# One pool for every tile, u through SyncE, and the first logits mixed with the last inverse in an attention-plus-S4 kernel

## The chip, the cores and the metric

The kernel runs on one core of a Trainium2 chip. Its time is device microseconds of one execution. The core has TensorE (PE; PEld is its weight load), VectorE (DVE), ScalarE (ACT), GpSimd (POOL) and SyncE (SP), each with an instruction stream of its own, and 16 DMA engines. DMAs are issued here from the queues of SyncE, ScalarE and GpSimd.

## What is computed

Two independent parts share one output of 2048 x 1280; the left 640 columns come from A, the right 640 from B.

```python
# A: local dilated attention; H = 32 heads of Dh = 20, window W = 8, dilation 2
q, k, v = split(x @ wqkv)                  # x 2048 x 640, wqkv 640 x 1920
idx = pos[:, None] - 2 * arange(8)[None]   # masked where negative
logits = einsum("hsd,hswd->hsw", q, k[idx]) * Dh ** -0.5
o = einsum("hsw,hswd->hsd", softmax(logits), v[idx])
a = o @ wo
# B: S4 convolution; D = 640 channels, N = 192 states, L = 2048
dt = exp(log_dt)
K[d, l] = real(sum_n C[d, n] * exp(dt[d] * A[d, n] * l) * dt[d] * B[d, n])
y = irfft(rfft(pad(u)) * rfft(pad(K)))[:L] + u * Dskip
```

## The kernel before, in words

Part B goes by five chunks of 128 channels (NCH = 5, 32 channels in each of four groups). For each chunk the coefficients are brought into base, log magnitude and phase (`prep_coef`, `prep_chunk`), written to a scratch in DRAM (`scr`) and read back transposed as "pieces" PF and PM (`load_pieces`). `table_steps` multiplies the pieces with constant matrices RF and RM, and ACT turns the results into tables of sines and exponentials Y and X; `kgen_steps` multiplies Y with X into the convolution kernel (tile Ksb). Each chunk does this in two halves, th = 0 and 1. `fwd_steps` is a two-step FFT by matmuls (f1 with BD, f2 with WU for u or WK for the kernel), run for u (`u_steps`, result stored to Udram) and for Ksb. `inv_steps` reloads u's spectrum as U and Uw, multiplies it with the kernel's (`prod`, L425) and makes the first step of the inverse (`ia`, L434) into Z. The second step, `ib` (L574), needs the Z of all five chunks: four are stored to Zdram and read back into the 40 KB tile Zall, the fifth is written there directly. It starts each PSUM tile with u times Dskip through an identity matmul, and puts the result where u was, from where two DMAs of four parts store it.

Steps are Python closures; `interleave` mixes two lists evenly. A scheduler of the framework then orders each engine's instructions by that order and by its own estimate of when they become ready; the result is a fixed stream for each engine. `InOrder` pins chains by hand: `order` on ACT, `vorder` on DVE, `sorder` on SyncE's loads of pieces and constants. PSUM has eight banks: in part B one tile "w" of two banks for the FFT steps (one buffer), "tb" of two banks (two buffers) for tables, "k" of one bank (two buffers).

Part A: `headA` loads x, transposes it with matmuls (L638) and projects the keys (L646), both beside the last inverse and `ib`. After part B's pools close, `partA` projects half the queries (L673), then mixes the logits of that half (DVE products at L695, matmuls at L698) with the projection of the values (L682), projects the other half of the queries, makes the first softmax (L716 to L733) and the second half's logits, then the weighted values (DVE L749, matmuls L753) and the output projection (L765). An item of logits takes eight window offsets w for one half of each 512 positions.

SBUF is divided into pools that open and close: `bbase` (u, WK, IA, H), `tabc`, `piece`, `tabA`, `prep`, then `tabB`, `a_h`, `zall`, `a_w`, `a_s`. A pool that opens in the place of a closed one waits until the closed one's tiles are done.

At the start ACT's queue issues log_dt (L51), two coefficient loads (L487), BD and the four parts of u (L492); the Exp of log_dt (L59) follows them in ACT's stream, and all coefficient work follows that Exp.

Of the kernel before, what the change touches and what calls it, by code (L numbers as in the profile page):

```python
# [44 lines left out]
def load_dt(tc, pools, prm):  # L45
    nc = tc.nc
    pool = pools["bbase"]
    ldt = pool.tile([128, NCH], bf16, name="ldt")
    lsrc = prm["B_log_dt"].rearrange("(g c t) -> g t c", g=4, c=NCH, t=32)
    for g in range(4):  # L50
        nc.scalar.dma_start(out=ldt[32 * g:32 * g + 32, :], in_=lsrc[g])  # L51
    return ldt


def prep_dt(tc, pools, ldt, order):
    nc = tc.nc
    pool = pools["bbase"]
# [9 lines left out]
def prep_coef(tc, pools, nat, lndt, n, order, vorder, pool, sfx):  # L67
# [5 lines left out]
    T = pool.tile([128, 5, n, CW], f32, name="cf" + sfx)  # L73
# [11 lines left out]
    def logs():  # L85
        order(nc.scalar.activation(out=T[:, 2:5], in_=T[:, 2:5], func=ACT.Ln, bias=pools["tiny"][:]))
        V.tensor_tensor(out=T[:, 3], in0=T[:, 3], in1=T[:, 2], op=A.subtract)
        V.scalar_tensor_tensor(out=T[:, 2], in0=T[:, 3], scalar=-1.0, in1=T[:, 3], op0=A.mult, op1=A.max)
        V.scalar_tensor_tensor(out=T[:, 4], in0=T[:, 4], scalar=0.5, in1=lndt.unsqueeze(2).to_broadcast(W), op0=A.mult, op1=A.add)
        order(nc.scalar.activation(out=T[:, 2], in_=T[:, 2], func=ACT.Exp, scale=-0.5))  # L90
        nc.scalar.activation(out=T[:, 3], in_=T[:, 3], func=ACT.Sign)
        nc.scalar.activation(out=T[:, 0:2], in_=T[:, 0:2], func=ACT.Sign, bias=pools["tiny"][:])
# [7 lines left out]
    return zed, logs, angle, T[:, 4], T[:, 2]  # L100


def prep_chunk(tc, pools, Are, Aim, dts, lam, ang, c, scr, vorder):
# [4 lines left out]
    pool = pools["prep"]  # L108
    st = {}

    def frac(out, x, q):
        tk = pool.tile([128, CW], f32, name="tk", tag="tk", bufs=2)
        V.tensor_scalar(out=tk[:], in0=x, scalar1=1.0 / q, scalar2=MAGIC, op0=A.mult, op1=A.add)
        V.tensor_scalar(out=tk[:], in0=tk[:], scalar1=MAGIC, scalar2=q, op0=A.subtract, op1=A.mult)
        V.tensor_tensor(out=out, in0=x, in1=tk[:], op=A.subtract)

    def base():
        b1 = st["b1"] = pool.tile([128, 3, CW], f32, name="b1", tag="b1", bufs=2)
        pc = pool.tile([128, 6, CW], f16, name="pc1", tag="pc1")
        tq = pool.tile([128, CW], f32, name="tq", tag="tq", bufs=2)  # L120
        first = V.tensor_scalar(out=b1[:, 1], in0=Are, scalar1=dts[:, 0, c:c + 1], scalar2=-60000.0, op0=A.mult, op1=A.max)
        second = V.tensor_scalar(out=tq[:], in0=Aim, scalar1=dts[:, 1, c:c + 1], scalar2=None, op0=A.mult)
        frac(b1[:, 0], tq[:], 65536.0)
        frac(b1[:, 2], b1[:, 0], 1024.0)
        nc.scalar.copy(out=pc[:, 0:3], in_=b1[:])
        vorder(first)
        vorder(second)
        lastop = V.tensor_tensor(out=pc[:, 3:6], in0=b1[:], in1=pc[:, 0:3], op=A.subtract)
        vorder(lastop)
        nc.sync.dma_start(out=scr[c, 0:6].rearrange("k p n -> p k n"), in_=pc[:])  # L130

    def logmag():
        pc = pool.tile([128, 2, CW], f16, name="pc2", tag="pc2")
        nc.scalar.copy(out=pc[:, 0], in_=lam)
        vorder(V.tensor_tensor(out=pc[:, 1], in0=lam, in1=pc[:, 0], op=A.subtract))
        nc.sync.dma_start(out=scr[c, 6:8].rearrange("k p n -> p k n"), in_=pc[:])

    def phi():
        tq = pool.tile([128, CW], f32, name="tq", tag="tq", bufs=2)
        b2 = pool.tile([128, CW], f32, name="b2", tag="b2")  # L140
        pc = pool.tile([128, 2, CW], f16, name="pc3", tag="pc3")
        V.tensor_scalar(out=tq[:], in0=st["b1"][:, 0], scalar1=31.5, scalar2=None, op0=A.mult)
        V.scalar_tensor_tensor(out=tq[:], in0=ang, scalar=-TURN, in1=tq[:], op0=A.mult, op1=A.add)
        frac(b2[:], tq[:], 65536.0)
        nc.scalar.copy(out=pc[:, 0], in_=b2[:])
        V.tensor_tensor(out=pc[:, 1], in0=b2[:], in1=pc[:, 0], op=A.subtract)
        nc.sync.dma_start(out=scr[c, 8:10].rearrange("k p n -> p k n"), in_=pc[:])
# [3 lines left out]
def new_pieces(tc, pools):  # L151
# [3 lines left out]
    PF = pools["piece"].tile([128, 8, CW], f16, name="PF", tag="PF")  # L155
    PM = pools["piece"].tile([128, 8, CW], f16, name="PM", tag="PM")
# [36 lines left out]
def table_steps(tc, pools, R, P, th, order, Y, X, rows=(128, 128), vorder=None):  # L193
# [8 lines left out]
    pool, psp = pools["tab"], pools["psum"]  # L202
# [129 lines left out]
def const_tile(tc, pool, arr, name, eng, dt=bf16, order=None):  # L332
    t = pool.tile(list(arr.shape), dt, name=name)
    ins = eng.dma_start(out=t[:], in_=tc.nc.inline_tensor(arr if dt == bf16 else arr.astype(np.float16), name="c_" + name).ap())
# [34 lines left out]
def fwd_steps(tc, pools, BD, W, src_fn, banks, ev1, ev2, each=None, done=None):  # L369
# [3 lines left out]
    pool = pools["fwd"]  # L373
# [31 lines left out]
def inv_steps(tc, pools, IA, Ud, banks, ev, done, zdst=None):  # L405
# [3 lines left out]
    pool = pools["inv"]  # L409
# [17 lines left out]
    def ia(q):  # L427
        def run():
            if q == 0:
                st["Z"] = zdst[0] if zdst is not None else pool.tile([128, 128, 32], bf16, name="Z", tag="Z")[:]  # L430
# [5 lines left out]
            if q == 3 and done is not None:  # L436
# [5 lines left out]
def partB(tc, pools, prm, B_u, B_Dskip, out_b, open_head):  # L442
# [4 lines left out]
    with ExitStack() as outer:  # L447
        opened = lambda name, **kw: outer.enter_context(tc.tile_pool(name=name, **kw))
        dpool = opened("dram", bufs=1, space=bass.MemoryType.DRAM)
# [3 lines left out]
        psk = opened("psum_k", bufs=2, space=bass.MemoryType.PSUM)  # L453
        bbase = opened("bbase", bufs=1)
        fwp = opened("fwd", bufs=1)
        ivp = opened("inv", bufs=1)
        short = ExitStack()
        tcp = short.enter_context(tc.tile_pool(name="tabc", bufs=1))
        pcp = short.enter_context(tc.tile_pool(name="piece", bufs=2))
        tabA = short.enter_context(tc.tile_pool(name="tabA", bufs=1))  # L460
        pools.update(psum=psk, bbase=bbase, piece=pcp, fwd=fwp, inv=ivp, tab=tabA)
        order = InOrder(tc)
        vorder = InOrder(tc)
        sorder = InOrder(tc)
        tiny = bbase.tile([128, 1], f32, name="tiny")
        nc.vector.memset(tiny[:], 1e-36)
        pools["tiny"] = tiny
        u = bbase.tile([128, 64, 160], bf16, name="u")
        Yb = [tabA.tile([128, 2, 6, 64, 16], bf16, name="Y0")]
        Xb = [tabA.tile([128, 2, 6, 16, 32], bf16, name="X0")]  # L470
# [4 lines left out]

        def u_steps(c, ev=ev):
            return fwd_steps(tc, pools, BD, WU, (lambda t: u[:, :, 32 * c + t]), Banks(psk, tags), ev, ev,
                             done=(lambda S: nc.sync.dma_start(out=Ud[c], in_=S[:].rearrange("p g k t -> p (g k t)"))))
        with tc.tile_pool(name="prep", bufs=1) as pp:
            pools["prep"] = pp  # L480
            n0 = pp.tile([128, 6, 1, CW], bf16, name="nat0")
            nr = pp.tile([128, 6, NCH - 1, CW], bf16, name="natr")
            for a in (5, 4):
                nc.sync.dma_start(out=n0[:, a, 0], in_=psrc(a, 0))
            ldt = load_dt(tc, pools, prm)
            for a in (0, 2, 1, 3):
                (nc.sync if a < 2 else nc.scalar).dma_start(out=n0[:, a, 0], in_=psrc(a, 0))  # L487
            P = new_pieces(tc, pools)
            RM, RF = (const_tile(tc, tcp, x, nm, nc.sync, f16) for nm, x in zip(("RM", "RF"), table_consts_np()[::-1]))
            BD = const_tile(tc, bbase, cn["BD"], "BD", nc.scalar)  # L490
            for g in range(4):
                nc.scalar.dma_start(out=u[32 * g:32 * g + 32], in_=usrc[g])  # L492
            for c in range(1, NCH):
                for a in (0, 2, 1, 3):
                    (nc.sync if a in (1, 3) else nc.gpsimd).dma_start(out=nr[:, a, c - 1], in_=psrc(a, c))
            dts = prep_dt(tc, pools, ldt, order)
            zed0, logs0, angle0, lam0, ang0 = prep_coef(tc, pools, n0, dts[:, 2, 0:1], 1, order, vorder, pp, "0")
            zedr, logsr, angler, lamr, angr = prep_coef(tc, pools, nr, dts[:, 2, 1:NCH], NCH - 1, order, vorder, pp, "r")
            base0, logmag0, phi0 = prep_chunk(tc, pools, n0[:, 4, 0], n0[:, 5, 0], dts, lam0[:, 0], ang0[:, 0], 0, scr, vorder)
            base0()  # L500
            load_pieces(tc, P, scr, 0, (0,), sorder)
            WU = const_tile(tc, tcp, cn["WU"], "WU", nc.sync, order=sorder)
            for c in range(1, NCH):
                for a in (4, 5):
                    nc.gpsimd.dma_start(out=nr[:, a, c - 1], in_=psrc(a, c))
            zed0()
            logs0()
            logmag0()
            load_pieces(tc, P, scr, 0, (1,), sorder)
            zedr()  # L510
# [354 lines left out]
```

## Time and profile before

| | |
|---|---|
| median of 3 runs | 597.35 us (596.28 to 598.55) |
| the profiled execution | 597.83 us, span from first to last instruction 596.1 us |
| busy share of the span | PE 73%, DVE 70%, ACT 57%, POOL 6% |
| mean granted PE clock | 0.891 |
| DMA | 49.46 MB in 47898 packets, 37080 of them under 512 B |

The stretches, in us from the span's start: 0-33 loads; 33-85 preparation and the first table; 85-145 preparation of the other chunks, u's second and third FFT; 145-379 the loop over chunks 1 to 4; 379-442 last kernel FFT, last inverse, transposes of x and keys; 442-456 first queries; 456-488 first logits and values; 488-501 second queries and first softmax; 501-523 second logits; 523-575 weighted values; 575-596 output projection.

In the table of windows each row gives the length of a stretch, then the busy us of every engine with its number of instructions, the share of full clock that PE was granted, the mean busy share of the DMA engines and their GB/s. A line of waits names the engine and line that stood idle, what ended the wait, the total, the number and the longest.

### The profile page before, as it was taken

How to read it: one execution, taken by the hardware profiler on the slowest of the kernel's cores; microseconds unless marked ns; L12 is line 12 of the kernel's file. 1: busy time of each engine (PE TensorE's matmuls, PEld its weight loads, DVE VectorE, ACT ScalarE, POOL GpSimd, SP SyncE). 2: the span in 40 equal slices, each digit the busy share in tenths (PEclk: the TensorE clock that was granted, in tenths of full speed). 3: DMA queues.
4: the chain of work that ended last, by engine and by line, in shares of the span. 5: the costliest groups of instructions: out<-in, count | busy, mean ns of one | idle time of the engine just before them, and what ended most of it. 6: DMA issues, size and time to landing. Idle time of an engine off the chain costs nothing. (4 is left out here: it accounts for less than half of the span.)

```text
span 596.1 us, 15315 instructions
## 1 busy us (share of the span) xinstructions
PE 434.2 (73%) x6897; PEld 269.7 (45%) x6904; DVE 416.9 (70%) x510; ACT 339.3 (57%) x435; POOL 34.8 (6%) x48
## 2 busy tenths in 40 slices
PE   0014179559888988897989888778996995533887
PEld 0011146444455655664655455775653772210345
DVE  0056659957797789889894978373323767999990
ACT  0057748458959796979597868353323554111355
POOL 7600000001000100010000000000000000000000
PEclk9999998759989999999998969979998998555699
DMA  8962055432000720171007000993343000000012
GB/s 137 133 106 83 1 229 148 141 94 94 12 2 17 222 82 2 36 208 76 2 1 214 2 1 1 286 417 140 70 84 83 2 6 2 0 1 2 24 58 101
DMA packets 47898, 49.46 MB, mean 83 GB/s; under 512 B 37080, under 2 KB 44184, under 8 KB 44504
## 3 DMA queue, kind: packets, MB, share of 16 engines
q1 hardware_dynamic: 37312, 44.84, 25.1%
q10 hardware_dynamic: 9368, 2.79, 3.5%
q0 software_dynamic: 1152, 0.85, 1.1%
q8 instruction: 54, 0.88, 0.6%
q14 instruction: 12, 0.10, 0.1%
HBM read 31.25 MB, written 17.14 MB: 81 GB/s over the span
## 5 line engine op out<-in xcount | busy, mean ns | idle before, releaser
L384 PE MATMUL ps_f<-BD,u 128*64 128x128 bf16 x320 | 23.2, 298 | 62.2 <-DMA u<-in_B_u_dram 40.0
L256 ACT ACTIVATE X<-ps_t 128x1024 bf16<-128x1024 int16 x60 | 60.6, 1043 | 10.0 <-PE ps_t L210 9.1
L256 ACT ACTIVATE Y<-ps_t 128x1024 bf16<-128x1024 int16 x60 | 59.4, 1041 | 1.9 <-PE ps_t L210 1.4
L210 PE MATMUL ps_t<-RF,PF 128*128 128x512 f16 (+1 forms) x160 | 53.4, 430 | 7.5 <-ACT X L256 3.3
L695 DVE TENSOR_TENSOR prod<-qT,kT 128x5120 bf16<-128x5120 bf16 x16 | 44.3, 2820 | 18.9 <-DMA wo<-in_A_wo_dram 14.4
L294 PE MATMUL ps_k<-Y,X 128*32 128x64 bf16 x1280 | 51.1, 295 | 1.7 <-issue 1.2
L384 PEld LDWEIGHTS <-u 128*64 128x64 bf16 x320 | 21.1, 206 | 66.2 <-issue 66.0
L749 DVE TENSOR_TENSOR prod<-v,attn 128x2048 bf16<-128x2048 bf16 (+1 forms) x48 | 46.9, 1034 | 1.6 <-PE ps_o L753 1.6
L297 PE MATMUL ps_k<-Y,X 64*32 64x64 bf16 x1280 | 46.9, 291 | 1.5 <-DVE Y L264 1.4
L345 DVE CAST A<-ps_f 128x1024 bf16<-128x1024 f32 x28 | 34.1, 1220 | 14.2 <-PE ps_f L384 14.1
L294 PEld LDWEIGHTS <-X 128*32 128x32 bf16 x1280 | 34.7, 110 | 18.0 <-issue 10.8
L297 PEld LDWEIGHTS <-X 64*32 64x32 bf16 x1280 | 34.6, 110 | 17.4 <-issue 15.5
L345 ACT CAST Ssp<-ps_f 128x1024 bf16<-128x1024 f32 x26 | 26.1, 1018 | 28.5 <-PE ps_f L395 21.9
L262 DVE TENSOR_TENSOR Y<-Y,M 128x2048 bf16<-128x2048 bf16 x30 | 36.6, 1219 | 4.4 <-ACT Y L256 4.3
L753 PE MATMUL ps_o<-prod,ident 32*32 32x512 bf16 (+1 forms) x768 | 23.2, 458 | 21.3 <-DVE prod L749 21.3
L264 DVE TENSOR_TENSOR Y<-Y,M 128x2048 bf16<-128x2048 bf16 x30 | 36.6, 1221 | 0.4
L268 DVE TENSOR_TENSOR X<-X,MX 128x2048 bf16<-128x2048 bf16 x30 | 36.6, 1218 | 0.4 <-ACT X L256 0.3
L230 ACT ACTIVATE M<-ps_t 128x1024 bf16<-128x1024 f32 x30 | 30.0, 1026 | 10.1 <-DVE Y L264 4.3
L210 PE MATMUL ps_t<-RM,PM 128*128 128x256 f16 (+4 forms) x120 | 23.8, 305 | 11.9 <-ACT E L223 5.2
L698 PE MATMUL ps_l<-prod,Gs 128*32 128x256 bf16 x320 | 16.4, 352 | 20.6 <-DVE prod L695 20.6
L213 PE MATMUL ps_t<-RF,PF 128*64 128x512 f16 (+1 forms) x160 | 25.8, 396 | 5.2 <-ACT Y L256 2.8
L434 PE MATMUL ps_ia<-IA,U 128*128 128x128 bf16 x160 | 24.9, 236 | 5.4 <-DVE U L425 2.3
(150 smaller groups left out, 824.5 us busy)
## 6 DMA issues: line engine op xcount, KB each, us to landing
Udram<-Ssp SPq DMA_DIRECT2D x5, 1024.0 KB
U<-Udram SPq DMA_DIRECT2D x5, 1024.0 KB
Uw<-Udram SPq DMA_DIRECT2D x10, 512.0 KB
Zdram<-Z SPq DMA_DIRECT2D x4, 1024.0 KB
Zall<-Zdram SPq DMA_DIRECT2D x4, 1024.0 KB
u<-in_B_u_dram ACTq DMA_DIRECT2D x4, 640.0 KB
xn<-in_A_x_dram SPq DMA_DIRECT2D x4, 640.0 KB
out_dram<-ob SPq DMA_DIRECT2D x16, 160.0 KB
```

Source lines behind the costliest of these rows:

```text
L210: MM(ps, lhsT=Pt[0:K, 2 * blk + th, 0:128], rhs=rhs[0:K], start=True, stop=True, skip_group_check=True)
L230: order(nc.scalar.activation(out=M[:, 2 * b:2 * b + 2, 0:4:3], in_=ps[:].rearrange("p i (k x) -> p i k x", k=2), func=ACT.Exp))
L256: order(nc.scalar.activation(out=dst, in_=ps[:].bitcast(i16)[:, :, 0::2], func=ACT.Sin, scale=SINSC))
L262: V.tensor_tensor(out=hi, in0=lo, in1=m(0), op=A.mult)
L264: V.tensor_tensor(out=lo, in0=lo, in1=m(2), op=A.mult)
L268: V.tensor_tensor(out=xf, in0=xf, in1=mx, op=A.mult)
L294: MM(o, lhsT=X[:, r, g, t], rhs=Y[:, r, g, :, t], start=(k == 0 and r == 0), stop=False, tile_position=(0, 32 * g), skip_group_check=True)
L297: MM(o, lhsT=X[hb:hb + 64, r, 4 + g % 2, t], rhs=Y[hb:hb + 64, r, 4 + g % 2, :, t], start=False, stop=(r == 1), tile_position=(hb, 32 * g) ...
L345: ins = self.nc.scalar.copy(out=out, in_=in_) if e == "a" else self.nc.vector.tensor_copy(out=out, in_=in_)
L384: MM(ps[64 * r:64 * r + 64, i], lhsT=src_fn(8 * q + i), rhs=BD[:, r], start=(i % 4 == 0), stop=True, skip_group_check=True, tile_position= ...
L695: V.tensor_tensor(out=pr[:], in0=q4[:, :, :, 256 * hf:256 * hf + 256], in1=k4[:, :, :, 256 * hf:256 * hf + 256], op=A.mult)
L749: V.tensor_tensor(out=p2[:, 0:nd], in0=v2[:, 8 * b:8 * b + nd, off:off + 256], in1=at[:, w, :].unsqueeze(1).to_broadcast([128, nd, 256]), ...
```

## The change

All SBUF tiles come from one pool, `arena`, and take each other's place by tags: x and the queries in the place of Y0, the keys in that of Y1, the preparation's scratch in those of Uw and Z, H in that of A1, and so on. ACT's queue issues log_dt only; the six loads of chunk 0's coefficients, then u, BD and the constants go through SyncE, u and BD after the pieces of the first two kinds, before those of the phase (`phi0`). ident is loaded through GpSimd. Ln of all chunks is taken before the first Exp of the tables (`lnr`, then `exp0`); the other chunks' Exp after the magnitudes (`expr`). The preparation's scratch is one tile for b1 (two places), tk, tq and b2 (one each), and the outgoing pieces have two places each. x is loaded and transposed in the stage of chunk 4's second table, in 12 steps through "w". Keys and queries are projected by halves of each 512 positions: the first halves (and 14 further columns of the keys) beside the last kernel FFT and inverse, the second halves of the keys with `ib` and the first logits, those of the queries after them. The fifth Z is stored to DRAM like the others, and `ib` reads all five back in six pieces of 12 rows, in two alternating places. `ib` takes three rows and one PSUM bank a step, was six and two. The values are projected beside the second logits and the first softmax. Weighted values and output projection keep their steps.

```diff
@@ partB, the start
-            for a in (0, 2, 1, 3):
-                (nc.sync if a < 2 else nc.scalar).dma_start(out=n0[:, a, 0], in_=psrc(a, 0))
-            BD = const_tile(tc, bbase, cn["BD"], "BD", nc.scalar)
-            for g in range(4):
-                nc.scalar.dma_start(out=u[32 * g:32 * g + 32], in_=usrc[g])
...
+        base0()
+        load_pieces(tc, P, scr, 0, (0,), sorder)
+        zed0()
+        ln0()
+        logmag0()
+        load_pieces(tc, P, scr, 0, (1,), sorder)
+        zedr()
+        lnr()
+        exp0()
...
+        for st in fills[:6]:
+            st()
+        expr()
+        angle0()
+        angler()
...
+        for g in range(4):
+            sorder(nc.sync.dma_start(out=u[32 * g:32 * g + 32], in_=usrc[g]))
+        BD = const_tile(tc, ar, cn["BD"], "BD", nc.sync, order=sorder)
+        phi0()
+        load_pieces(tc, P, scr, 0, (2,), sorder)
+        WU = const_tile(tc, ar, cn["WU"], "WU", nc.sync, order=sorder)
@@ partB, the last chunk and the end
+                    else:
+                        att.load_x()
+                        work += att.transposes(lambda: psk.tile([128, 2, 512], f32, name="ps_xt", tag="w", bufs=1))
...
+        att.load_w()
+        interleave(work[8:] + prev_ia, att.proj_k(0, kbank, evh) + att.proj_q(0, kbank, evh))
+    psa = pools["open_psum_a"]()
+    H = const_tile(tc, ar, cn["H"], "H", nc.sync, tag="A1")
+    NP = 12
...
+            if l % NP == 0:
+                np_ = min(NP, 64 - l)
+                zt[0] = z = ar.tile([128, NCH, 2 * NP, 32], bf16, name="zq", tag=("Ssp", "WK")[l // NP % 2])
+                for c in range(NCH):
+                    nc.sync.dma_start(out=z[:, c, 0:2 * np_], in_=Zd[c, :, 64 * l:64 * (l + np_)].rearrange("p (m t) -> p m t", t=32))
...
+            evy(u[:, l:l + n, :].rearrange("p b c -> p (b c)"), ps[:, 0:160 * n])
...
+    att.run(psa, [ib(l) for l in range(0, 64, 3)])
@@ Attention.run
+        rest = self.proj_k(1, new, ev)
+        interleave([self.logits(0, w) for w in range(W)], other + rest)
+        for st in self.proj_q(1, new, ev):
+            st()
+        self.wo = ar.tile([128, 5, D], bf16, name="wo4", tag="WU")
...
+        self.v2 = ar.tile([128, DH, HALO + 512], bf16, name="v2", tag="u")
+        sm = self.softmax(0)
+        sm[0]()
+        l1 = []
+        for w in range(W):
+            l1.append(self.logits(1, w))
+            if w % 2 == 0:
+                l1.append(sm[1 + w // 2])
+        interleave(l1, [self.proj_v(d) for d in range(DH)])
...
+        self.o4 = ar.tile([128, 4, 5, 512], bf16, name="o4", tag="Y0")
```

## The prediction

> **What bounds the kernel now.** I read the table of windows first, cut where the work changes, then the waits and the timeline of the two places in it where engines idle. Columns: stretch, length, then busy us with counts for PE, PEld, DVE, ACT and POOL, granted PE clock, DMA share, GB/s.
>
> ```profile
> 0.00:33.00 33.00, 0.00 (x0) 0.00 (x0) 0.06 (x1) 1.42 (x2) 21.30 (x30) 1.00 0.88 131
> 33.00:85.00 52.00, 19.47 (x132) 10.38 (x132) 33.30 (x61) 31.21 (x38) 0.00 (x0) 1.00 0.34 94
> ...
> 340.00:379.00 39.00, 34.59 (x647) 23.56 (x639) 28.46 (x36) 24.51 (x28) 0.00 (x0) 0.87 0.16 49
> 379.00:442.00 63.00, 54.15 (x920) 37.96 (x915) 29.57 (x38) 24.70 (x34) 0.16 (x1) 0.92 0.59 194
> 442.00:456.00 14.00, 11.22 (x51) 4.97 (x51) 0.00 (x0) 5.35 (x11) 0.32 (x1) 1.00 0.65 140
> 456.00:488.00 32.00, 28.81 (x562) 21.36 (x562) 23.76 (x10) 13.73 (x25) 0.50 (x7) 0.89 0.01 3
> 488.00:501.00 13.00, 10.72 (x50) 4.76 (x49) 9.46 (x8) 8.90 (x13) 0.00 (x0) 1.00 0.07 5
> 501.00:523.00 22.00, 8.80 (x140) 5.13 (x140) 22.00 (x10) 1.79 (x3) 0.00 (x0) 0.52 0.01 1
> ```
>
> No single engine bounds the whole. Nothing computes for 33 us. From 85 to 379 (rows not all shown) the table and FFT loop keeps PE 86% busy and DVE 82%, and the change barely touches it. From 379 to 523 the stages alternate: PE-bound with DVE half idle (63 us), a bubble with no DVE work (14 us), PE-bound (32 and 13 us), then DVE-bound with PE at 40% (22 us). The waits of the first 45 us, with total, times and longest, and the timeline there (start, length, engine, line):
>
> ```profile
> DVE dts L61 <- ACT dt L59: 32.2, 1, 32.2
> ACT L59 <- DMA u<-in_B_u_dram: 31.6, 1, 31.6
> ```
> ```profile
> 5.71 25.83 ACTq L492 DMA_DIRECT2D u<-in_B_u_dram  x4
> 31.57 1.28 ACT L59 ACT_TABLE_LOAD   x1 [31.57 <-DMA u<-in_B_u_dram]
> 40.01 1.18 PE L384 MATMUL ps_f<-BD,u 128*64 128x128 bf16 x16 [40.01 <-DMA u<-in_B_u_dram]
> ```
>
> The four u issues occupy ACT's queue until 31.54, and the first activation, which needs only the 0.3 KB ldt issued by 2.71, stands behind them. Everything follows that activation. The bubble at 442-456 is named by the waits of 379-523: the new pool's tiles take the place of u, which is still being stored.
>
> ```profile
> ACT qT L674 <- DMA out_dram<-u: 8.5, 1, 8.5
> DVE prod L695 <- DMA wo<-in_A_wo_dram: 14.4, 1, 14.4
> ```
>
> **The change, part 1: the start.** u moves from ACT's queue to SyncE's, pinned behind the pieces of the first two kinds. The first activation then waits only for ldt. Its landing isn't shown. Bounds: 1.9 us after issue (the PM pieces, issued by 41.69 after which PE used them at 43.51) to 6.6 us (the Dskip loads in the page's DMA part), so 4.6 to 9.3; I take 7, 24.6 us earlier than 31.57. From there to the second set of pieces took 31.57 to 50.10, 18.5 us; 1.7 of it was WU's load ahead of the second scratch write (4.8 us from issue to landing against 3.1 for the first), and WU now comes later. So u is issued at 7 + 16.8 = 24. It is 2.62 MB, and 20:40 moved 131 GB/s at a DMA share of 0.94, so 20 us: u lands at 44-46, six us later than the 40.0 of before. BD, phi's pieces, WU, WK and IA are queued on SyncE behind u. If the issue holds SyncE for the 25.8 us it held ACT, phi's pieces leave at 50; they are not ready before 47 anyway (first Sin 67.95 - 24.6 - 2, the two reorders of logs and exponentials sparing two table loads of 1.28, is 41; the scratch write of phi came 6.1 us after that Sin). With 4.4 us to PE's use (74.09 to 78.48) the first Sin of X can run at 52-55, against 79.5. u's eight FFT steps then run from 46; bare, eight such steps took 117.06 to 131.85 and an eviction of 1.2, 16 us, so they end at 62-64, against 86. DVE's order puts the other chunks' preparation behind these steps (84.9 before). Gain 21 to 24 by this, 14 if u holds its queue for all 25.8 us and lands at 52, at most 26 if nothing new is late. I take 20, since Ln of all chunks now stands ahead of the first table Exp and costs some of it back, and the preparation's scratch is single (tk, tq, b2), which DVE's in-order stream covers.
>
> A rule speaks against this part. The Trainium skill, page "DMA: Bandwidth & Descriptors", section "Issuing engines are not separate DMA queues", says that choosing another issuing engine saves only sequencer time, "usually small relative to the DMA itself". By it this part would be worth about nothing and the total would be 577. The row measures the sequencer time at 25.83 us, and I go by the row.
>
> **Part 2: the loop.** Its tiles keep their buffer counts under new tags; Uw and Y1 wait for the preparation's scratch and coefficients, as the pools did; behind Uw's load (128.74) SyncE holds pieces issued from 142.95 on, for a chunk whose table starts at 200.6: time to spare. I cost 85-340 at 0 (a reordered schedule can give 4 either way; nothing in the rows has a sign).
>
> **Part 3: x transposed in the last loop stage.** 80 matmuls (8.0 us busy at L638) and 20 evictions move from 390-405 into or just behind 340-379, where PE idles 4.4 us, DVE 10.5 and ACT 14.5. They are 12 steps through the one "w" bank, behind four inverse steps that took 357 to 373. x can load only when Y0 is free (K copied at 364.0) and 2.6 MB at the 361 GB/s of 380:400 take 7 us, so the steps begin near 368 and at the bare 2 us each end near 395, over K's own FFT (379-390, where PE now idles for evictions). I charge 2 us to the loop and half of PE's 8 us to the next stage. If stage A had no other PE work to cover the rest, it would be 16 us more (373 to 395 against 379).
>
> **Part 4: 379 to 523, 144 us before.**
> - Stage A, K's FFT and last inverse with half the keys and queries. PE: FFT 5.1 (L384 2.2, L395 2.9), inverse 5, 20 projection parts of 1.1 (8.58 us for 39 matmuls at L646) 22, halos 1 (25 narrow ones; as 64-column rows at 0.03-0.06 each), transposes 4: 37. ACT now takes all 25 projection evictions, 15 us of 0.59, beside its 10 there: hidden. The three weight loads and H (3.4 MB, 10 us at 361 GB/s) lie under the same 37; late ones would cost up to those 10. Of 63 us in 379:442 PE idled 9; I keep 5. It ends at 421.
> - Stage B, last inverse (ib) with the first logits. PE: ib 11 x 1.46 = 16, rest of keys 11, logits 8 x 0.55 = 4.4: 31.5. DVE: 8 products of 2.77 = 22.2 and 11 evictions of 0.69: 30. The stage 456:488 was busy on PE to 90%, so 35. Z is now stored whole and read back. A 1 MB store took 86.30 to 89.90, 3.6 us, before its reader was issued; five loads at 0.45 issue and a landing of 2 to 4 make 9-10 us for the first group, behind A's projections. Later groups have two places and 6.5 us of work to hide 1 MB (2.9 us at 361 GB/s). The first half of the output, 1.3 MB in 320 B rows, is 10 us of DMA in front of one group: I charge 3. B ends at 459.
> - Stage C/D, other queries, then second logits, first softmax and values together. PE: 11 + 20 x 1.08 + 4.4 = 37, at 90% 41. DVE: 22.2 + 11.1 of softmax = 33, under it. u's store (9 us, 441.9 to 450.8) is hidden by the query projection before v2 takes its place. Ends at 500.
> Before, the values ran without softmax and the second logits without values; that is where 23 us come from, with the bubble. With part 3's 2, tail gain 21. Bounds: 33 if PE is 100% busy in B to D and stage A loses nothing (37 + 31.5 + 3 + 37 = 108.5 of 144, less the 2); 5 if each stage loses what 379:442 lost (9 in 63, 7 us more in all) plus an exposed first Z group of 9.
>
> Weighted values and output (523-596) keep their instructions: 0. The halo copy of v2 now comes just ahead of their second step; a landing of 2-4 us with softmax work beside it: 0, else 3.
>
> **Sum.** Profiled execution 597.83 (span 596.1, 1.7 around it) - 20 - 21 = 556.8; it lies 0.5 above the median 597.35, so 556.
>
> **Rivals.**
> 1. Start only: the single bank and the Z round trip eat the tail gain. For: one "w" bank took 4 us a step at 357-373; 12 x 4 = 48 us. Against: those steps shared ACT with Sin. 597.35 - 20 = 577.
> 2. Tail only: u's 25.8 us on SyncE hold back phi's pieces and WU as they held ACT. For: SyncE has ten issues queued behind. Against: these are ready late. 597.35 - 21 = 576.
> 3. Slower: the Z stream isn't read ahead. Six groups, each of five loads on SyncE, stand behind the store of u or behind the group before. A Zall load held SyncE 0.43 to 2.15 us; five at 1.1 and 3.6 landing are 9 us, 54 in all if exposed: 597.35 - 41 + 54 = 610. It decides from 41/6 = 6.8 us exposed per group. Against: two places, and keys and logits that don't need Z.
> 4. The move of u doesn't free ACT because ldt itself lands late: against it stands 0.3 KB issued at 2.71. It falls under 2.
>
> **How the numbers follow.** Measurement tells 0.5% from no change. Both gains 0.66; rival 1 0.12; rival 2 0.10; rival 3 0.08, of which a quarter lands within 0.5%; other losses as large as both gains, 0.04, a quarter of it too within 0.5%. Faster 0.66 + 0.12 + 0.10 = 0.88, same 0.03, slower 0.09. The range holds the main case (597.35 - 26 - 33 = 538 to 597.35 - 14 - 5 = 578) and rivals 1 and 2 with a little for their own spread: 538 to 580.
>
> **What would show it.** Right: the first ACT activation at 5-9 us, u<-in_B_u_dram issued by SPq near 24, first matmul on u near 46, base of chunk 1 near 64; ps_xt before 400; products of logits beside ps_ib, DVE over 80% busy there; ps_v beside the second logits with the clock near 1.0 instead of 0.52; the first weighted value near 480. Wrong: long PE or DVE waits on zq or on out_dram<-u, a first activation after 15 us, or the loop's period (56 us, E of first halves at 144.7 and 200.6) changed by over 2 us.

## The result, and the profile after

The changed kernel takes 570.54 us (median of 4 runs, 566.64 to 575.34) beside 597.86 for the kernel before on the same chip: a ratio of 0.9525, 95% interval 0.9464 to 0.9586. That is faster and inside the predicted range, but by 27 us where 41 were forecast. Times are medians of all executions, while the ratios leave out those more than 1.5% above the fastest of the same kernel (575.34 here, 562.39 and 563.12 with the late store alone, where 562.39 is the profiled one). The profiled execution took 571.97 us, its span is 570.2.

The start first: waits of the first 45 us (total, times, longest), then the timeline (start, length, engine, line) with the idle time before each row. In the changed kernel u's load is L502, the base's first matmul L376.

```profile
DVE dts L61 <- ACT dt L59: 6.5, 1, 6.5
```
```profile
5.84 1.28 ACT L59 ACT_TABLE_LOAD   x1 [5.84 <-DMA ldt<-in_B_log_dt_dram]
...
25.31 10.30 SPq L502 DMA_DIRECT2D u<-in_B_u_dram  x4
...
43.99 1.19 PE L376 MATMUL ps_f<-BD,u 128*64 128x128 bf16 x16 [6.44 <-DMA BD<-c_BD]
```

The first activation now waits for log_dt alone and runs at 5.84 instead of 31.57; DVE's wait of 32.2 us has become 6.5. The same four loads of u that held ACT's queue for 25.83 us hold SyncE's for 10.30, and the first matmul on u comes at 44.0. The table of windows, in the same columns as before, from the loop's last stage on:

```profile
320.00:362.00 42.00, 35.15 (x641) 24.57 (x641) 29.88 (x38) 26.05 (x29) 0.00 (x0) 0.92 0.58 178
362.00:400.00 38.00, 34.62 (x303) 20.46 (x303) 11.75 (x15) 22.10 (x36) 0.16 (x1) 0.96 0.25 84
400.00:424.00 24.00, 19.55 (x539) 13.61 (x539) 21.63 (x14) 5.66 (x10) 0.22 (x3) 0.86 0.53 155
424.00:448.00 24.00, 16.27 (x125) 7.35 (x123) 8.32 (x6) 6.53 (x12) 0.28 (x4) 0.93 0.31 81
448.00:466.00 18.00, 14.39 (x177) 7.10 (x176) 9.80 (x10) 10.70 (x16) 0.00 (x0) 0.91 0.28 60
466.00:500.00 34.00, 26.72 (x576) 23.00 (x576) 27.74 (x13) 13.07 (x24) 0.32 (x1) 1.00 0.17 34
```

Stage A (362:400) is nearly full on PE, 34.6 of 38 us. The mixing of logits and `ib` works for 24 us (400:424): DVE is busy 90%, PE 81%. Then comes a hole that the sum didn't have: from 424 to 448 PE is busy 68% and DVE 35%. The waits of 362 to 500 name what ends its idle times:

```profile
POOL v L810 <- DMA out_dram<-u: 25.5, 1, 25.5
...
DVE prod L706 <- ACT kT L337: 14.3, 2, 9.6
```

SyncE's queue, and the rows of PE that belong to it (L577 the matmuls of `ib` with the identity, L583 those with H, L654 the projections):

```profile
418.73 4.54 SPq L590 DMA_DIRECT2D out_dram<-u  x4
423.36 7.84 SPq L572 DMA_DIRECT2D zq<-Zdram  x10
...
461.25 4.49 SPq L590 DMA_DIRECT2D out_dram<-u  x4
```
```profile
423.53 1.00 PE L577 MATMUL ps_ib<-u,ident 128*128 128x160 bf16 x12
...
425.12 0.45 PE L577 MATMUL ps_ib<-u,ident 128*128 128x160 bf16 x4
...
434.21 1.44 PE L654 MATMUL ps_qk<-xa,wk 128*128 128x512 bf16 x3 [0.65 <-ACT kT L337]
...
436.98 0.81 PE L654 MATMUL ps_qk<-xa,wk 128*128 128x512 bf16 x3 [0.65 <-ACT kT L337]
...
457.14 2.39 PE L583 MATMUL ps_ib<-zq,H 32*32 32x160 bf16 x128
```

Read together: at 418.7 the first half of u's result goes out, and the last two groups of Z stand behind it on SyncE. PE has run the identity part of the last six `ib` steps by 425.5, so six of the eight PSUM banks are open. The bank of the last two logits is a seventh, from 431.2 until ACT fetches it at 444.4; between them the key parts go at 1.9 us each, most with a wait for a kT eviction before them, and before and after at 1.08. The 128 H matmuls that close the six banks come late in PE's fixed order, at 457, among the second-half queries. By then it is not Z that they wait for: the DMA engines have moved nothing between 433 and 446.

```profile
433.00:446.00 13.00, 8.78 (x50) 3.46 (x49) 3.60 (x2) 3.84 (x7) 0.14 (x2) 0.88 0.00 0
```

The last query is evicted at 465.3, the second half's first product starts at 465.9, and v is evicted from 479.2. The wait of 25.5 us for u's store, long as it is, holds nothing up: v2's place is free at 470.7, and ACT, whose order has a fetch of the second logits first, evicts v 8.5 us later.

```profile
465.29 0.58 ACT L337 CAST qT<-ps_qk 128x512 bf16<-128x512 f32 x1 [0.49 <-PE ps_qk L654]
465.91 8.30 DVE L706 TENSOR_TENSOR prod<-qT,kT 128x5120 bf16<-128x5120 bf16 x3 [4.72 <-ACT qT L337]
...
470.73 0.32 POOL L810 MEMSET v<- 32x280 bf16 x1 [25.54 <-DMA out_dram<-u]
...
478.75 0.60 ACT L721 ACTIVATE lsb<-ps_l 128x512 f32<-128x512 f32 x1 [3.73 <-PE ps_l L709]
479.25 4.99 ACT L695 CAST v<-ps_v 128x512 bf16<-128x512 f32 x10
```

The weighted values run without a break from 500.1.

### The profile page after: what moved, and what is told of

Its sections match the earlier page's. It is cut to its first block, busy times and chain, and to the rows that moved or that the text cites. A ratio compares the mean times of both kernels' runs of the same rounds, so it can differ in the third digit from the quotient of the medians.

```text
span 570.2 us, 15418 instructions
## 1 busy us (share of the span) xinstructions
PE 430.1 (75%) x6929; PEld 266.7 (47%) x6929; DVE 410.3 (72%) x501; ACT 342.3 (60%) x449; POOL 35.2 (6%) x49
## 4 chain that ended last, share of the span: by engine, by line
PE 29%; DVE 9%; ACT 7%; issue 6%; DMA 2%; SPq 0%; ACTq 0%; POOL 0%; DVEq 0%
PE ps_qk L654 7%; PE ps_v L693 4%; DVE prod L763 3%; PE ps_k L289 3%; PE ps_op L781 2%; DVE prod L706 2%; PE ps_k L286 2%; PE ps_ib L583 2%; ACT Y L248 2%; PE ps_l L709 2%; ACT X L248 1%; PE ps_ia L426 1%; PE ps_t L202 1%; PE ps_xt L634 1%; PE ps_ib L577 1%
## 5 line engine op out<-in xcount | busy, mean ns | idle before, releaser
L706 DVE TENSOR_TENSOR prod<-qT,kT 128x5120 bf16<-128x5120 bf16 x16 | 44.7, 2822 | 25.1 <-ACT kT L337 14.3
L202 PE MATMUL ps_t<-R,PF 128*128 128x512 f16 (+1 forms) x160 | 51.8, 421 | 8.4 <-ACT X L248 3.7
L289 PE MATMUL ps_k<-Y,X 64*32 64x64 bf16 x1280 | 47.7, 291 | 4.4 <-issue 2.4
L202 PE MATMUL ps_t<-R,PM 128*128 128x256 f16 (+4 forms) x120 | 23.4, 299 | 33.0 <-DMA PM<-scr 22.5
L376 PE MATMUL ps_f<-BD,u 128*64 128x128 bf16 x320 | 23.1, 296 | 22.9 <-DVE A L337 10.3
L376 PEld LDWEIGHTS <-u 128*64 128x64 bf16 x320 | 20.8, 204 | 27.3 <-issue 27.1
L205 PE MATMUL ps_t<-R,PF 128*64 128x512 f16 (+1 forms) x160 | 25.4, 384 | 5.5 <-ACT Y L248 3.4
L202 PEld LDWEIGHTS <-PM 128*128 128x128 f16 (+1 forms) x120 | 8.6, 102 | 42.8 <-DMA PM<-scr 22.5
L337 DVE CAST Ssp<-ps_f 128x1024 bf16<-128x1024 f32 x14 | 17.1, 1220 | 12.6 <-PE ps_f L387 12.6
```

Source lines behind the costliest of these rows:

```text
L202: MM(ps, lhsT=Pt[0:K, 2 * blk + th, 0:128], rhs=rhs[0:K], start=True, stop=True, skip_group_check=True)
L289: MM(o, lhsT=X[hb:hb + 64, r, 4 + g % 2, t], rhs=Y[hb:hb + 64, r, 4 + g % 2, :, t], start=False, stop=(r == 1), tile_position=(hb, 32 * g) ...
L337: ins = self.nc.scalar.copy(out=out, in_=in_) if e == "a" else self.nc.vector.tensor_copy(out=out, in_=in_)
L376: MM(ps[64 * r:64 * r + 64, i], lhsT=src_fn(8 * q + i), rhs=BD[:, r], start=(i % 4 == 0), stop=True, skip_group_check=True, tile_position= ...
L706: self.nc.vector.tensor_tensor(out=pr[:], in0=q4[:, :, :, hs], in1=k4[:, :, :, hs], op=A.mult)
```

## The experiments

The times are medians; ratios are to the kernel before, run on the same chip.

**u through SyncE alone**, in the kernel before:

```diff
-            BD = const_tile(tc, bbase, cn["BD"], "BD", nc.scalar)
-            for g in range(4):
-                nc.scalar.dma_start(out=u[32 * g:32 * g + 32], in_=usrc[g])
...
+            for g in range(4):
+                sorder(nc.sync.dma_start(out=u[32 * g:32 * g + 32], in_=usrc[g]))
+            BD = const_tile(tc, bbase, cn["BD"], "BD", nc.sync, order=sorder)
```

(WU's load also goes behind phi's pieces.) Expected: 

> The kernel before, with only u and BD moved from ACT's queue to SyncE's, behind the pieces of the first two kinds, and WU behind those of the phase; pools, order of logs and scratch as before. Theory (the queue): ACT's first activation at 5 to 9 us instead of 31.6, u's first spectrum stored near 64 instead of 86, first E of chunk 1 at 122 to 124 (144.7 before, 116.2 changed), total 22 us under the kernel before: 576. Rival (the shared scratch with two places, and Ln ahead of Exp, made the gain at the start): spectrum stored after 80, total 590 or more. If the first E of chunk 1 comes at 116, the further 6.6 us between the first and second table half also come from the queue.

Measured: 576.79 us, 0.9673 (0.9627 to 0.9719), 20 us less. Chunk 1's first table starts at 123.4 instead of 144.7. The queue is the cause of the start's 20 us. The changed kernel reaches the same point at 116.2: from chunk 0's second table to there it takes 41.0 us, the kernel before and this one 47.7. Those further 6.7 us come with the rewritten preparation, not with the queue; which part of it, no run here separates.

**u back on ACT's queue**, in the changed kernel (the same four loads and BD issued by `nc.scalar` ahead of the coefficients). Expected: 

> The changed kernel, with u and BD back on ACT's queue at the place they had before. Theory (the queue): 22 us are lost again, u's first spectrum stored near 86, total near 592, under the kernel before by what the scratch and the tail bring (5 to 6). Rival (scratch and order): total within 6 us of the changed kernel's 570.

Measured: 595.70 us, 0.9989 (0.9953 to 1.0025). All the rest of the change together, new pool, half projections, Z by DRAM, mixed logits, is worth nothing that can be measured when u stays on ACT. The move of u is worth 25 us inside the changed kernel (28 by the ratios), and the tail's forecast 21 are missing here too.

**Second-half keys after the first logits**, in the changed kernel:

```diff
-        interleave([self.logits(0, w) for w in range(W)], other + rest)
-        for st in self.proj_q(1, new, ev):
+        interleave([self.logits(0, w) for w in range(W)], other)
+        for st in rest + self.proj_q(1, new, ev):
```

Expected: 

> The changed kernel, with the ten second-half key parts after the first logits instead of mixed among them. Theory: the last two first-half products wait for key evictions that they don't read (14.3 us of waits of the products on the keys' evictions); these waits go, the eight products end near 425 instead of 443.6, softmax follows beside the key and query projections, total 5 to 12 us under the changed kernel: 558 to 565. Rival: PE is the bound of the stage, the parts only move: within 3 us of 570.

Measured: 565.14 us, 0.9459 (0.9400 to 0.9518). The eight products run in 28 us without a wait for kT, against 44 before the edit. But the last six `ib` steps still come at 455 to 459, and v from 468.8. The ratio falls by 0.0066, 4 us, which the two intervals don't tell from nothing: the wait for kT is at most a part of the loss.

**u's stores from GpSimd's queue** (L590 by `nc.gpsimd`). Expected: 

> The changed kernel, with the two stores of u's result issued from GpSimd's queue instead of SyncE's. Theory: the last two groups of Z reads stand behind the first store on SyncE, and the six last inverse steps, begun by their identity matmuls at 423.5, hold six of eight PSUM banks until 457; without the store ahead of them they run by 432, the key parts take 1.1 us each instead of 1.9, the second store ends 20 us earlier, the values' evictions start near 460: 8 to 15 us less, 555 to 562. Rival: the reads are late because of their own size and latency; PE waits for them in the same place, total within 3 us of 570.

Measured: 575.11 us, 0.9636 (0.9597 to 0.9676): slower by 5 than the changed kernel, against expectation. Its waits between 415 and 450 have

```profile
PEld L583 <- DMA zq<-Zdram: 7.5, 1, 7.5
```

The Z group issued at 414.4 landed near 426 although no store stood ahead of it on its queue: store and reads were in flight together, and PE stood still for these reads. The place behind a store on the queue is thus not the only thing that can make them late. The last `ib` step came early (433.3), but the framework's scheduler had put the first softmax behind the second logits (its last step at 494 instead of 457.5), so this run doesn't price the early steps.

**The transposes of x moved from the loop into stage A:**

```diff
-                        work += att.transposes(lambda: psk.tile([128, 2, 512], ...))
...
-        interleave(work[8:] + prev_ia, att.proj_k(0, ...) + att.proj_q(0, ...))
+        interleave(work[8:] + prev_ia, att.transposes(...) + att.proj_k(0, ...) + att.proj_q(0, ...))
```

Expected: 

> The changed kernel with the twelve transpose steps of x taken out of the loop's last stage and interleaved with the last inverse and the half projections instead. If the transposes cost the loop TensorE time and nothing else, the last stage falls from 44.8 us to about 40 (4.3 us of the transposes' 7.4 us lay in it), the stretch from the last Ksb to the first product of the logits grows from 37.6 to about 41 to 42, since TensorE is busy for 34 of its 38 us, and the time stays at 568 to 573. If they held the loop up in another way (PSUM banks, evictions on DVE and ACT), the last stage falls to 37 to 39, stage A grows by 3 or less, and the time comes to 565 to 567.

Measured: 579.41 us, 0.9705 (0.9663 to 0.9747). The loop's last stage falls to 37.7 us from 44.8, but the stretch from the last Ksb to the first product grows from 37.6 to 53.7; both theories missed that. In the loop's last stage itself the second theory was right: 7.0 us less, where only 4.3 us of the transposes' PE time lay in it. The windows of this run (loop's last stage, transposes, projections):

```profile
315.00:353.00 38.00, 33.52 (x649) 23.23 (x643) 28.29 (x36) 24.18 (x29) 0.00 (x0) 0.96 0.42 143
353.00:379.00 26.00, 16.55 (x166) 11.58 (x162) 8.78 (x9) 8.61 (x11) 0.16 (x1) 0.67 0.34 80
```

From 353 to 379 the twelve steps pass one by one through their single bank, at 2 us each, and most projections, which need all of x, come behind: PE is busy 64%. Beside the loop the same steps cost 7 us; they are well placed there.

**A third place for the streamed Z, alone, with the keys after the logits, and with the transposes moved as well:**

```diff
-                zt[0] = z = ar.tile([128, NCH, 2 * NP, 32], bf16, name="zq", tag=("Ssp", "WK")[l // NP % 2])
+                zt[0] = z = ar.tile([128, NCH, 2 * NP, 32], bf16, name="zq", tag=("Ssp", "WK", "Uw")[l // NP % 3])
```

Expected, alone: 

> The changed kernel with a third place for the streamed Z (the one of the inverse's second input, free by then), so that groups three to five are issued on SyncE before the first store of u and only the last, of four blocks, behind it. If the late Z is what holds the last six eviction steps until 457 and, through the PSUM banks and the second store, the v evictions until 479, these steps run by about 432, key parts take 1.1 us rather than 1.9, the v evictions start by about 466 to 470 and the time is 558 to 564. If the loss in this stage is the products' wait for the key evictions alone, the steps come early but products seven and eight still come at 428 to 440, and the time stays at 567 to 571.

Expected, with the keys after: 

> Both: a third place for Z, and the ten second-half key parts after the first logits. If the two causes are separate, the eight products run within 26 us (as with the keys after alone: 28 us), the last eviction steps are done by about 430, v evictions start by 465, and the time is 554 to 560. If they are one cause seen twice, the time is that of the better of the two alone, 562 to 566.

Expected, with the transposes too: 

> All three edits: third place for Z, keys after the first logits, transposes in stage A rather than in the loop. If the transposes only move TensorE time, within 2 us of the run with the first two edits; if they hold the loop up in another way, 3 to 5 us less.

Measured: alone 566.10 us, 0.9473 (0.9426 to 0.9520), 3 us by the ratios, which the intervals don't tell from nothing. Twenty `ib` steps were done by 424, but the last group, four blocks, still stood behind the store, and the last steps came at 452. With two banks open instead of six the key parts no longer wait for evictions. But the seventh and eighth products still wait for kT until 427.8 and 438.1, as the second branch of the expectation has it, and the second half's first product stands behind the softmax on DVE until 457.9:

```profile
460.73 1.26 PE L709 MATMUL ps_l<-prod,Gs 128*32 128x256 bf16 x20 [6.50 <-DVE prod L706]
```

So the open banks alone don't make the loss. With the keys after: 556.97 us, 0.9302 (0.9259 to 0.9345), v from 465.0; the two edits together bring 13 us, and either alone 3 to 4. With the transposes moved too: 566.66, 0.9484 (0.9450 to 0.9518): they cost 10 us in this form as well, where 2 more or up to 5 less were expected.

**The first store emitted behind Z**, alone, with the keys after, and with the third place as well:

```diff
-            if l in (30, 63):
-                a0, a1 = (0, 33) if l == 30 else (33, 64)
+            if l in (60, 63):
+                a0, a1 = (0, 33) if l == 60 else (33, 64)
```

Expected, alone: 

> The changed kernel with the first store of u emitted with step 60 rather than step 30, so that on SyncE three of its four parts stand behind all of Z; Z keeps its two places and the keys stay among the logits. If SyncE's order is what made the last Z late, the last six eviction steps come at about 427 to 435 instead of 457 to 461, the key parts take 1.1 us, the products still wait for key evictions, the v evictions start by about 468 to 472, and the time is 560 to 566. If the small packets of the store on the DMA engines were the cause, they come just as early, since the store now follows; if it is the Z reads' own rate, the steps come no earlier than 440.

Expected, with the keys after: 

> The same late store, with the second-half keys after the first logits; Z in two places. If the third place only helped because it let Z be read ahead of the store, this gives what the third place with the keys after gave, 554 to 560; if reading further ahead is needed too, the last steps come after 435 and the time is 559 to 564.

Expected, all three: 

> Third place, keys after, and the late store. With the third place and the keys after alone, the last step (one block) was evicted at 452.7, u's second store went out at 453 and the v evictions began at 465. If that last step is what still holds them, it now comes at about 430, the second store is done by 442, the v evictions start at 453 to 458, and the time is 546 to 552. If TensorE and the second-half queries (done at 449) bound this stretch, the v evictions start at 460 or later and the time stays at 554 to 558.

Measured: alone 558.55 us, 0.9312 (0.9273 to 0.9351). SyncE's queue and PE's row in this run:

```profile
418.57 7.60 SPq L572 DMA_DIRECT2D zq<-Zdram  x10
426.23 10.27 SPq L590 DMA_DIRECT2D out_dram<-u  x7
```
```profile
427.06 2.39 PE L583 MATMUL ps_ib<-zq,H 32*32 32x160 bf16 x128
```

The last 128 H matmuls run at 427.1 instead of 457.1, and everything behind follows. The ratio falls by 0.0213 from the changed kernel's; with the two intervals put together (0.0061 and 0.0039, root of the sum of squares 0.0072) that is 8 to 17 us, about what was missing (14), for one statement emitted ten `ib` steps (30 rows) later. The place of the store is thus shown to be the cause. The run moves the store out of the queue's way and off the DMA engines at once, and with it the framework's whole order, so it doesn't separate these. With the keys after as well 556.32 us, 0.9305 (0.9271 to 0.9338); with all three edits 559.58, 0.9349 (0.9305 to 0.9393). None of these differs from the store's move alone by more than the intervals allow, and neither does the third place with the keys after: these are repairs of one loss, not gains to be added. The last expectation, 546 to 552, failed by the reason that its second branch gives, though the time lies above that branch's 554 to 558 too: the last step did come at 433.8, but PE and the second-half queries bound the stretch, and v came at 470.7. The windows of the run with the late store and the keys after show it:

```profile
397.00:421.00 24.00, 18.28 (x544) 12.77 (x547) 22.54 (x14) 6.15 (x11) 0.36 (x5) 0.93 0.47 140
421.00:450.00 29.00, 27.17 (x304) 14.06 (x293) 16.16 (x15) 16.36 (x27) 0.47 (x3) 1.00 0.66 150
450.00:485.00 35.00, 28.02 (x576) 23.71 (x576) 27.41 (x13) 13.08 (x25) 0.00 (x0) 0.95 0.03 4
```

DVE is 94% busy, then PE 94%, and the hole is gone.

**One place for Z** (`tag="Ssp"`), to price the rival in which it isn't read ahead. Expected: 

> The changed kernel with one place for the streamed Z instead of two, so that no group is read before the last product with the group before it: the price of the rival in which Z is not read ahead. By that rival's sum each of the five later groups exposes its read, which took 4 to 7 us in the trace after, so 20 to 35 us more than the changed kernel, 590 to 605. If TensorE and VectorE have enough other work here (key and query parts, logits), half of it or less shows: 575 to 585.

Measured: 575.30 us, 0.9629 (0.9583 to 0.9675), 5 us over the changed kernel; the intervals just touch. The waits of 395 to 480:

```profile
PE ps_ib L583 <- DMA zq<-Zdram: 15.1, 4, 9.7
```

PE waits 15 us for Z by name, and a third of that reaches the end.

## Why the prediction was right or wrong

Gains by stage, in us of the profiled executions: what the sum said, what the changed kernel shows, and the run with the late store and the keys after.

| stretch | predicted | changed | late store, keys after |
|---|---|---|---|
| start to chunk 1's first table | 20 | 28.5 | 27.7 |
| loop, to the last Ksb | -2 | -11.5 | -8.8 |
| A, to the first product | 35 | 39.3 | 40.7 |
| B to D, to the unbroken run of weighted values | -12 | -33.5 | -22.2 |
| values and output, to the last output issue | 0 | 3.5 | 4.0 |
| sum | 41 | 26.3 | 41.4 |

- **Part 1, the start: mechanism right, size low.** The activation came at 5.84 (7 predicted), u's issue at 25.3 (24), the first matmul at 44.0 (46), chunk 1's base by 64.3 (62 to 64). The queue alone gave 20 us, as summed. The term missed the 6.7 us of the new preparation, which had been counted as a cost ("Ln of all chunks ... costs some of it back"). The Trainium skill's rule (page "DMA: Bandwidth & Descriptors", section "Issuing engines are not separate DMA queues") that another issuing engine saves little is answered by two runs: 0.9673 with the move alone, 0.9989 with everything but the move. The row of 25.83 us was the better guide, since what it held up was ACT's own stream.
- **Parts 2 and 3, the loop: -2 was too small.** The transposes ran from 343.5 to 369.6, not from 368 to 395 as summed, so more of them lies in the loop. Its last stage grows by 5.7 us (39.0 to 44.7), and moving the transposes out shortens it by 7.0. That is more than the 4.3 us that they take on PE there; what the rest is, no run shows. The first stage of chunk 1 adds 1.9 us (24.1 against 22.2, in every kernel with the new pool) and that of chunk 3 adds 3.9, which not every execution has (last section); the other stages together change by less than 0.1.
- **Part 4, stage A: right**, 37.6 us against 42; PE 34.6 busy against the 37 counted.
- **Part 4, stage B: the step that failed.** It says of the first store "10 us of DMA in front of one group: I charge 3". The row of SyncE has it in front of two groups, which leave 5 us later for it, and the charge left out what goes with that: banks opened by the identity matmuls, and H matmuls that PE's order has at 457, some 24 us after the last Z had come. Moving that store took 13 us off the end (8 to 17), where 3 had been charged. Which of these links weighs most stays open: freeing most of the banks alone brought 3 us, and the keys' move alone 4.
- **Part 4, B to D: too short by about 10 us even so.** With the store moved and the keys behind, the products and `ib` end 38 us after the first product, as the sum had it, but the sum had 11 us of key parts in that stage. From first product to weighted values this run needs 88.8 us against 79. PE is busy 73.5 us of the 88 in the windows above, against 68.5 counted, and waits for the first products and the second-half queries.
- **The total in range is in part luck.** In the changed kernel the start's extra 8.5 us stand against 21 forecast for the rest, which in fact loses 2.2. That the best run's 41.4 meets the 41 is chance as well, since its rows miss theirs by 4 to 10 us, up and down.
- **Rivals.** Rival 1 (start only) came true in its result, though not with its price: nothing was gained behind the start. The Z round trip ate into the tail gain, but with its place behind a store, and the transposes through one bank did so by 7 us, not 48. Rival 2 (SyncE held by u) is ruled out by the first two runs. Rival 3 was priced too high: a fully serial Z costs 5 us more than the changed kernel, not the 54 of its sum, since keys, queries and logits fill most of the wait. In the changed kernel PE waits for Z by name for 1.6 us only, while the matmuls on the late Z stand in its stream some 24 us behind the landing.
- **The signs named in advance** held but for three: DVE over 80% busy beside `ib` only until 424; the weighted values, whose first came at 483.3 but whose run began at 500.1; and the loop's period, which changed by 1.7 us at the place named but by 3.9 around chunk 3. The long wait on out_dram<-u, 25.5 us, is POOL's, not PE's or DVE's, and was followed by 8.5 us of slack.

The late store with the keys after the logits (556.32) beats both the kernel before and the changed one; the single moved store (558.55) does nearly all of it.

## What to carry to other kernels

An issuing queue that also computes is a resource: price a DMA issue by the row that shows how long it holds its engine, and by what stands behind it there. Where stores and reads share a queue, follow the order in which they are emitted to the last reader: a store that nothing waits for belongs behind every read that something waits for. Price its cost by the chain behind the delayed read, too: here reads issued 5 us later went with a loss of 13. A long wait in the list costs something only if the work behind it starts when it ends. When several edits repair the same stretch, test them singly and together before adding their gains: here two that brought 3 and 4 us alone brought 13 together, and one of them brought nothing beside a third.

## What was not expected of the hardware

The same four loads of u held a queue for 25.83 us when issued at 5.7 us on ACT, beside the preparation's loads, and for 10.30 (10.03 with the move alone) when issued at 25 us on SyncE; put back on ACT's queue in the changed kernel, at 4.1, they held it for 27.02. Whether the engine or the other traffic makes the difference was not separated.

In four of the profiled executions with the new loop (the changed kernel, u on ACT, the late store alone, all three edits) the first stage of chunk 3 takes 28.4 to 29.5 us; in the others 25.0 to 25.1, from the same code there. The changed kernel has, in waits and then in the timeline of that stage,

```profile
PE ps_f L376 <- issue: 2.5, 1, 2.5
```
```profile
237.68 0.71 PE L376 MATMUL ps_f<-BD,u 128*64 128x128 bf16 x8 [2.54 <-issue]
...
240.48 1.06 PE L387 MATMUL ps_f<-A,WU 128*128 128x128 bf16 x8
```

and the run with the late store and the keys after has in the same place

```profile
236.18 1.12 PE L376 MATMUL ps_f<-BD,u 128*64 128x128 bf16 x15
...
238.79 0.61 PE L387 MATMUL ps_f<-A,WU 128*128 128x128 bf16 x8
```

PE stops for 2.5 us (2.0 to 2.5 in the four) in the middle of sixteen like matmuls, for nothing that the profile shows, and eight matmuls just behind then take 1.06 us instead of 0.61; the stage's granted clock is 0.94 (0.88 with all three edits) instead of 1.00. The stage is 3.4 to 4.5 us longer in the executions that have it. What PE waits for there stays open.
